# A decode block at the DMA rate: six units of K by transfers of eight rows, the second gate half ahead of the first's transposes, one stationary down block

## The chip, the cores and the metric

One core of a Trainium2 chip runs the whole program. The metric is the device time in microseconds, from runs on the chip. A profile comes from one further execution, taken by the hardware profiler. Engines are named as the profile names them: PE multiplies matrices, PEld loads PE's weights, DVE, ACT and POOL are the vector, scalar and general engines, SP is the queue that issues almost all transfers here. Sixteen DMA engines carry the transfers.

## The reference, cut to what matters

Two residual layers, each applied twice: grouped attention on a cache of 32768 positions (batch 2, 32 query heads, 8 key/value heads of width 128), then a gated feed-forward part. All data are float32. The two caches are 268 MB each and both are read in full in each of the two layers, 1074 MB in all; the weights are read beside them, and the only output is the result of 2 x 512 values.

```python
def _A_ref(x, k_cache, v_cache, wq, wo):
    q = (lambda x, *d: x.transpose(*d))((x @ wq).reshape(B, Sq, Hq, Dh), 0, 2, 1, 3)
    k = jnp.repeat(k_cache, rep, axis=1)
    v = jnp.repeat(v_cache, rep, axis=1)
    scores = jnp.einsum("bhqd,bhkd->bhqk", q, k) * (Dh ** -0.5)
    p = _softmax(scores, axis=-1)
    o = jnp.einsum("bhqk,bhkd->bhqd", p, v)
    ...
def _B_ref(x, w_gate, w_up, w_down):
    h = _gelu(g) * u          # g = x @ w_gate, u = x @ w_up
    return jnp.einsum("bsf,fd->bsd", h, w_down)

x = x + _A_ref(_layernorm(x, axis=-1), ...)
x = x + _B_ref(_layernorm(x, axis=-1), ...)
x = x + _A_ref(...)
x = x + _B_ref(...)
```

## The kernel before

**Memory.** `M` is one SBUF tile of 110 units; a unit is 512 columns (2 KB) in all 128 partitions. Three slots of 32 units (`SLOT_A`, `SLOT_B`, `SLOT_C`) take the chunks of K and V in turn. Three places of four units (`PL[0]`, `PL[1]`, `PL[2]`) take weights in pieces of four units. `mem(u, n)` is units u to u + n. A chunk of K or V is a half of one head's sequence: 32 units, 128 rows of 64 KB.

**Transfers.** `chunk` and `stream` only write a plan (`add`): an ordered list of key, source, place and size. `pump` (L101) issues from the head of that list on SP as long as the place is free, and stops at the first entry whose place is still taken. It is called by each `free`, that is at the point of the program where PE has been given the last instruction that reads the units. The order of the transfers is thus the order of the plan, and an entry that waits holds all behind it. Each transfer waits on SP until PE is done with its place.

**A layer.** For each of the 16 pairs of head g and batch b: `scores` runs two K chunks against the query window (L286), DVE takes the peak, `softmax` makes the weights and transposes them on PE (L305 to L320), `values` runs two V chunks (L330), `combine` and `project` add the head to the residual in the PSUM bank `W`. Layer 1 takes the pairs in the reverse order, and starts with the pair that layer 0 ended with: of its K, most of chunk 0 and all of chunk 1 are still there.

**The feed-forward part** (`feedforward`, L352). `center` takes the mean out of `W`; `deviation` gets the variance (PE L254, DVE, then a power on POOL). Gate and up weights are 28 units in two halves: `v = 0` has four column groups (16 units), `v = 1` three (12 units), each with four matmul steps over k (L367). Each half has a bank of its own, `G[0]` (bank 5) and `G[1]` (bank 7). Then ACT and DVE make the gelu product `th` of the half (L381 to L389), PE transposes it with `selt` (L391), DVE copies it to `hT` (L392). Only then does PE start the other half. `restart` (L230) puts the residual into `W` again, and the down product adds 14 blocks of 128 rows: as the moving operand against `hT` (L401), in the last layer only the first 10, and the last four as the stationary operand (`tail = 4`, L416), so that the result comes out transposed and needs no further step. In between, `halves` copies `W` out on ACT and DVE, and L408 sums its groups.

**Between the layers.** Weights pass through the three places: gate and up in seven pieces, down in four, the next queries in eight. The query of head 7 comes first (`Q7`, bank 5), since its K chunk 1 is in SBUF: `deviation(X)`, scaling (`query_copy`, L263 and L264), gather (L271) and `window`; then for each other group gg four query units (L259) into bank 7 and four units of scores (L286), and the score units' places are released for the next K pieces.

Of the kernel before, what the change touches and what calls it, by code (L numbers as in the profile page):

```python
# [16 lines left out]
P = 128  # L17
NB = 2
# [3 lines left out]
KC = DM // P  # L22
# [3 lines left out]
FD = DF // P  # L26
# [18 lines left out]
KFREE = CH - NPS  # L45

# [23 lines left out]
def block_kernel(ctx: ExitStack, tc: tile.TileContext, x, consts, kt, vt, wq, wo, gu, wd, out):  # L70
# [27 lines left out]
    def add(key, src, u, n):  # L98
        plan.append((key, src, u, n))

    def pump():  # L101
        while plan:
            key, src, u, n = plan[0]
            if any(busy[u:u + n]):
                return
            plan.popleft()
            for i in range(u, u + n):
                busy[i] = True
            live[key] = u
            nc.sync.dma_start(mem(u, n), src)  # L110
# [24 lines left out]
    def chunk(name, l, g, b, h, base, cuts=(CH,), turn=0):  # L135
        src = (kt if name == "k" else vt)[b, g, h]
        lo = 0
        where = {}
        for n in cuts:
            u = base + (lo + turn) % CH  # L140
            add((name, l, g, b, h, lo), cols(src, lo, n), u, n)
# [19 lines left out]
    for l in range(2):  # L161
# [190 lines left out]
    def feedforward(l):  # L352
# [5 lines left out]
        s = 0  # L358
        G = [bank[5], bank[7]]
        g, u, a, th = [mem(U_PT + j // 2)[:, (j % 2) * FN:(j % 2 + 1) * FN] for j in range(4)]  # L360
        for v in range(2):
            nt = 4 if v == 0 else 3
# [13 lines left out]
            R = 32 * nt  # L376
# [12 lines left out]
            nc.vector.tensor_tensor(th[:R], a[:R], u[:R], op=OP.mult)  # L389
            for j in range(2):  # L390
                nc.tensor.matmul(G[v][:, j * 8:(j + 1) * 8], th[:, j * P:(j + 1) * P], selt, start=True, stop=True)  # L391
            nc.vector.tensor_copy(hT[:, v].rearrange("p j r -> p (j r)"), G[v][:, :16])  # L392
        restart()
        where = pieces[("wd", l)]
        tail = 4 if l == 1 else 0
        for n in range(FD - tail):
            key, un = where[n]
            at(key)
            r, j = divmod(n, 2)
            v, t = divmod(r, 4)  # L400
            nc.tensor.matmul(W[32 * (n % 4):32 * (n % 4) + NB, :], hT[:, v, j, 2 * t:2 * t + NB], mem(un),  # L401
                             start=(0 < n < 4), stop=(n + 4 >= FD - tail))
            free(un)
        if tail:
            ws = mem(U_PT + 1)
            halves(ws, W)
            for c in (2, 3, 0, 1):
                nc.tensor.matmul(X[:, c * NB:(c + 1) * NB], ws[:, c * P:(c + 1) * P], sel[:, :NB],  # L408
                                 start=(c == 2), stop=False)
            for n in range(FD - tail, FD):  # L410
                key, un = where[n]
                at(key)
                r, j = divmod(n, 2)
                v, t = divmod(r, 4)
                for c in range(KC):
                    nc.tensor.matmul(X[:, c * NB:(c + 1) * NB], mem(un)[:, c * P:(c + 1) * P],  # L416
                                     hT[:, v, j, 2 * t:2 * t + NB], start=False,
                                     stop=(n == FD - 1 and c == KC - 1))
# [68 lines left out]
    for gg in range(7):  # L487
# [4 lines left out]
        if gg == 5:  # L492
            take(PL[1], 4) if False else None
        free(where[4 * gg][1], 4)
        n = 4 if gg < 6 else CH - i
# [87 lines left out]
```

## Time and profile before

| what | value |
|---|---|
| runs (us) | 2603.39, 2609.26, 2610.44; median 2609.26 |
| profiled execution, its own time | 2602.04 us |
| its span | 2599.9 us, 20241 instructions |
| PE granted clock, mean | 0.735 |
| busy: PE, PEld, DVE, ACT, POOL | 53%, 16%, 6%, 3%, 0% |
| HBM read | 1102.93 MB, 424 GB/s over the span |
| SP's data queue (q1) | 26496 packets, 1102.86 MB, 98.5% of 16 engines |

The span is the stretch from the first to the last instruction of the profiled execution; its own time also holds what lies around it. The profile's slices of the span give 428 to 440 GB/s, but for the first (421), the two around the middle (367 and 352) and the last (272). A row of the windows' view has, after the stretch and its length, the busy time of PE, PEld, DVE, ACT and POOL with the number of instructions, then PE's granted clock, the DMA engines' mean busy share (of 16) and GB/s. A row of the chain has the start, the length and what was done or waited for. A float32 matmul stands in the profile as two records, in the program's order as one.

### The profile page before, as it was taken

To read this page: it belongs to the slowest core of one execution; us is meant where nothing else is said; L and a number is where in the kernel's file an instruction comes from. 1 tells how busy PE (TensorE), PEld (TensorE's weight loads), DVE (VectorE), ACT (ScalarE), POOL (GpSimd) and SP (SyncE) were. 2 spreads that over 40 slices of the span, in tenths; PEclk is the share of its full clock that TensorE was granted. 3 is DMA by queue.
4 is the path that set the end of the run, shared out by engine and by line. 5 is a ranking of instruction groups with operands and counts; after the bars stand their busy time and mean duration, and the time that the engine had idled before them with its cause. 6 is when DMAs were issued, how large, how long until landed. Compare 5 with 4: busy or idle time off the path is not lost.

```text
span 2599.9 us, 20241 instructions
## 1 busy us (share of the span) xinstructions
PE 1370.0 (53%) x9456; PEld 409.2 (16%) x9456; DVE 147.2 (6%) x433; ACT 73.1 (3%) x196; POOL 3.2 (0%) x12
## 2 busy tenths in 40 slices
PE   3544544554554456445576554555455454455556
PEld 1111111111111111111122111111111111111112
DVE  0000000000000000000011000000000000000001
ACT  0000000000000000000000000000000000000000
POOL 0000000000000000000000000000000000000000
PEclk9776777677677767767788777776777777777767
DMA  9999999999999999999899999999999999999996
GB/s 421 434 433 434 432 434 429 433 435 434 430 433 431 429 435 435 431 433 434 367 352 440 431 433 430 434 434 433 434 431 431 432 430 434 434 433 434 431 428 272
DMA packets 26867, 1104.23 MB, mean 425 GB/s; under 512 B 3232, under 2 KB 3360, under 8 KB 4128
## 3 DMA queue, kind: packets, MB, share of 16 engines
q1 hardware_dynamic: 26496, 1102.86, 98.5%
q8 instruction: 74, 1.21, 0.2%
q10 hardware_dynamic: 288, 0.09, 0.0%
q14 instruction: 9, 0.07, 0.0%
HBM read 1102.93 MB, written 0.00 MB: 424 GB/s over the span
## 4 chain that ended last, share of the span: by engine, by line
DMA 58%; PE 28%; another core or an unknown queue 12%; DVE 1%; issue 1%; ACT 1%; SPq 0%; POOL 0%; ACTq 0%; DVEq 0%; POOLq 0%
DMA M<-in_vt 50%; PE bank L330 16%; PE bank L286 8%; DMA M<-in_kt 6%; DMA cst<-in_consts 1%; PE bank L348 1%; PE bank L341 1%; PE bank L367 1%; PE bank L259 1%; DVE M L235 0%; PE bank L401 0%; ACT M L234 0%; PE bank L416 0%; PE bank L242 0%
## 5 line engine op out<-in xcount | busy, mean ns | idle before, releaser
L286 PE MATMUL bank<-M,qw 128*32 128x512 f32 x4096 | 582.3, 731 | 534.8 <-DMA M<-in_kt 534.8
L330 PE MATMUL bank<-M 128*16 128x512 f32 x4096 | 580.1, 730 | 530.9 <-DMA M<-in_vt 530.9
L286 PEld LDWEIGHTS bank<-M,qw 128*32 128x32 f32 x4096 | 142.2, 131 | 963.7 <-DMA M<-in_kt 575.3
L330 PEld LDWEIGHTS bank<-M 128*16 128x16 f32 x4096 | 137.2, 112 | 947.2 <-issue 947.1
L289 DVE TENSOR_REDUCE sm<-bank 128x1 f32<-128x512 f32 x64 | 44.3, 692 | 1107.1 <-PE bank L286 1107.1
L311 ACT ACTIVATE M<-bank,sm 128x512 f32<-128x512 f32 x64 | 43.4, 682 | 1229.3 <-DVE sm L306 1229.3
L235 DVE COPY M<-bank 128x256 f32<-128x256 f32 x33 | 14.0, 425 | 1117.6 <-ACT M L234 1117.6
L314 PE MATMUL bank<-cst,M 128*128 128x128 f32 x256 | 49.2, 335 | 40.6 <-ACT M L311 40.3
L341 PE MATMUL bank<-cst,M 128*128 128x4 f32 x256 | 33.8, 255 | 30.4 <-DVE M L235 30.4
L315 DVE COPY M<-bank 128x512 f32<-128x512 f32 x64 | 43.8, 692 | 60.7 <-PE bank L314 60.7
L234 ACT COPY M<-bank 128x256 f32<-128x256 f32 x33 | 12.3, 372 | 1162.0 <-PE bank L330 1155.2
L314 PEld LDWEIGHTS bank<-cst,M 128*128 128x128 f32 x256 | 34.9, 169 | 51.6 <-ACT M L311 51.6
L341 PEld LDWEIGHTS bank<-cst,M 128*128 128x128 f32 x256 | 31.0, 191 | 59.9 <-DVE M L235 59.9
L305 PE MATMUL bank<-cst,sm 128*128 128x128 f32 x32 | 10.3, 323 | 35.0 <-DVE sm L304 35.0
L348 PE MATMUL bank<-M,oT 128*2 128x512 f32 x128 | 21.1, 736 | 4.1 <-DVE oT L343 4.1
L259 PE MATMUL bank<-M,xw 128*32 128x512 f32 x128 | 21.2, 777 | 3.7 <-DMA M<-in_wq 3.0
L319 PEld LDWEIGHTS bank<-cst,sm 128*128 128x128 f32 x128 | 21.8, 240 | 0.0
L367 PE MATMUL bank<-M,xw 128*32 128x512 f32 x112 | 20.4, 785 | 2.1 <-DMA M<-in_gu 1.6
L319 PE MATMUL bank<-cst,sm 128*128 128x4 f32 x128 | 20.1, 263 | 0.0
L230 PE MATMUL bank<-cst,xin 128*2 128x128 f32 x40 | 6.0, 301 | 23.4 <-DMA cst<-in_consts 23.4
L305 PEld LDWEIGHTS bank<-cst,sm 128*128 128x128 f32 x32 | 4.2, 133 | 64.1 <-DVE sm L304 64.1
L311 ACT ACTIVATION_READ_ACCUMULATOR M<-bank,sm 128x1 f32 x64 | 12.5, 196 | 0.0
(70 smaller groups left out, 150.4 us busy)
## 6 DMA issues: line engine op xcount, KB each, us to landing
M<-in_wo SPq DMA_DIRECT2D x16, 1024.0 KB, 51.1
M<-in_vt SPq DMA_DIRECT2D x2, 6144.0 KB, 46.6
M<-in_wq SPq DMA_DIRECT2D x2, 4096.0 KB, 17.1
M<-in_gu SPq DMA_DIRECT2D x8, 1024.0 KB, 6.4
M<-in_wq SPq DMA_DIRECT2D x8, 1024.0 KB, 6.4
M<-in_kt SPq DMA_DIRECT2D x2, 4096.0 KB, 18.8
M<-in_kt SPq DMA_DIRECT2D x6, 1024.0 KB, 13.2
M<-in_gu SPq DMA_DIRECT2D x3, 2048.0 KB, 44.5
```

What stands on the lines that cost most here:

```text
L259: nc.tensor.matmul(Q[32 * k:32 * k + 32, :], xw[:, k, XO - 2 * g:XO - 2 * g + 32], mem(u), start=start, stop=stop)
L286: nc.tensor.matmul(S[32 * t:32 * t + 32, :], w[:, 28 - 4 * c:60 - 4 * c], mem(u), start=start, stop=stop)
L289: nc.vector.tensor_reduce(mx[:, h:h + 1], S, axis=AX.X, op=OP.max)
L305: nc.tensor.transpose(X[:, :P], nm.to_broadcast([P, P]), ident)
L311: nc.scalar.activation(p[h], S[h], AF.Exp, bias=bias, scale=SCALE, accum_out=ls[:, h:h + 1])
L314: nc.tensor.transpose(S[h][:, k * P:(k + 1) * P], p[h][:, k * P:(k + 1) * P], ident)
L315: nc.vector.tensor_copy(mem(U_PT + h), S[h])
L319: nc.tensor.matmul(X[:, P:P + REP], ls[:, h:h + 1].to_broadcast([P, P]), mask, start=(h == 0), stop=(h == 1))
L330: nc.tensor.matmul(acc[32 * t:32 * t + 16, :], mem(U_PT + h)[:, k * P + 32 * t + 16 * e:k * P + 32 * t + 16 * e + 16], mem(u), start=(h == ...
L341: nc.tensor.matmul(X[:, :REP], md[:, c * P:(c + 1) * P], sel[:, 4 * c:4 * c + 4], start=(c == 2), stop=(c == 1))
L348: nc.tensor.matmul(W[32 * t:32 * t + NB, :], oT[:, t, :], mem(u + t), start=(t > 0 and g == orders[l][0][0]), stop=(g == orders[l][-1][0]))
L367: nc.tensor.matmul(G[v][32 * t:32 * t + 32, :], xw[:, k, XO:XO + 32], mem(un), start=(k == 0), stop=(k == KC - 1))
```

## The change

It has four parts.

1. `LOW` names two K chunks per layer. For them `pump` issues the transfer as three: rows 0 to 111, 112 to 119 and 120 to 127. In each layer one chunk is named whole (32 units) and of the other only its first half (16 units); 16 rows of 48 units are as many bytes as 128 rows of six units. The bytes and places are the same.
2. `feedforward` gives PE the products of the second half before the transposes of the first. The restart, the first transposes, eight down blocks, the second transposes and the other blocks follow.
3. In the last layer one down block, not four, is the stationary operand (`tail = 1`), and it comes before the sum over `W`'s groups.
4. Between the layers the variance of the query goes to `W` and not to `X`, so that the first other group's query units run before the gather of head 7; scores follow from the second group on, five units a time.

```diff
+LOW = [{(3, 1): (CH,), (6, 0): (CH // 2, CH // 2)}, {(4, 0): (CH,), (1, 1): (CH // 2, CH // 2)}]
...
-            key, src, u, n = plan[0]
+            key, src, u, n, rows = plan[0]
...
-            nc.sync.dma_start(mem(u, n), src)
+            lo = 0
+            for m in rows:
+                nc.sync.dma_start(mem(u, n)[lo:lo + m], src[lo:lo + m])
+                lo += m
...
-            chunk(nm_, l, g, b, h, ring[i % 3], (24, 4, 4) if last else (CH,))
+            cuts, rows = (CH,), (P,)
+            if last:
+                cuts = (24, 4, 4)
+            elif nm_ == "k" and h == 0 and (g, b) in LOW[l]:
+                cuts, rows = LOW[l][(g, b)], (P - 16, 8, 8)
+            chunk(nm_, l, g, b, h, ring[i % 3], cuts, rows=rows)
...
+        products(0)
+        gelu(0)
+        products(1)
+        restart()
+        hidden(0)
+        gelu(1)
+        down(0, 8)
+        hidden(1)
+        down(8, FD)
         if tail:
             ws = mem(U_PT + 1)
             halves(ws, W)
+            for n in range(FD - tail, FD):
+                key, un = below[n]
+                at(key)
+                for c in range(KC):
+                    nc.tensor.matmul(X[:, c * NB:(c + 1) * NB], mem(un)[:, c * P:(c + 1) * P], part(n),
+                                     start=(n == FD - tail and c == 0), stop=False)
             for c in (2, 3, 0, 1):
                 nc.tensor.matmul(X[:, c * NB:(c + 1) * NB], ws[:, c * P:(c + 1) * P], sel[:, :NB],
-                                 start=(c == 2), stop=False)
+                                 start=False, stop=(c == 1))
...
-    deviation(X)
+    deviation(W)
     query_copy(Q7, mem(U_PT))
-    query_gather(mem(U_PT), Q7, 7, 1)
-    w = window(g, b)
...
+        if gg == 0:
+            query_gather(mem(U_PT), Q7, 7, 1)
+            w = window(g, b)
+            continue
+        n = 5 if gg < 6 else CH - i
```

`products`, `gelu` and `hidden` are the three pieces of the old loop over `v` (L362 to L375, L376 to L389, L390 to L392) as functions; `down(lo, hi)` is the loop of L396 to L403 over blocks lo to hi, up to the stationary ones.

PE, the feed-forward part of layer 0 and the start of layer 1. Before (bank_79 is bank 5, bank_80 `W`, bank_81 bank 7, also called `X`; L242 and L244 belong to `center`, L254 is the variance):

```order
L367 MATMUL bank_79<-M,xw 32x512 x12
L391 MATMUL bank_79<-cst,M 128x8 x2
L367 MATMUL bank_81<-M,xw 32x512 x12
L391 MATMUL bank_81<-cst,M 128x8 x2
L230 MATMUL bank_80<-cst,xin 2x128 x4
L401 MATMUL bank_80<-M,hT 2x512 x14
L242 MATMUL bank_81<-cst,M 128x4 x4
L244 MATMUL bank_81<-cst,sm 128x16 x2
L259 MATMUL bank_79<-M,xw 32x512 x4
L254 MATMUL bank_81<-sm 128x2
L271 MATMUL bank_79<-cst,M 128x2 x4
L259 MATMUL bank_81<-M,xw 32x512 x4
```

Now (line numbers of the changed kernel: L379 is L367 before, L407 L391, L242 the restart, L422 L401, L271 L259, L266 L254, L283 L271):

```order
L379 MATMUL bank_79<-M,xw 32x512 x12
L379 MATMUL bank_81<-M,xw 32x512 x12
L242 MATMUL bank_80<-cst,xin 2x128 x4
L407 MATMUL bank_79<-cst,M 128x8 x2
L422 MATMUL bank_80<-M,hT 2x512 x8
L407 MATMUL bank_81<-cst,M 128x8 x2
L422 MATMUL bank_80<-M,hT 2x512 x6
L254 MATMUL bank_81<-cst,M 128x4 x4
L256 MATMUL bank_81<-cst,sm 128x16 x2
L271 MATMUL bank_79<-M,xw 32x512 x4
L266 MATMUL bank_80<-sm 128x2
L271 MATMUL bank_81<-M,xw 32x512 x4
```

The second half's products and the restart moved ahead of the first transposes, eight down blocks ahead of the second transposes, and (last row) the first other group's query units ahead of the gather, which stood in this place.

PE at the end of the program, before:

```order
L367 MATMUL bank_81<-M,xw 32x512 x12
L391 MATMUL bank_81<-cst,M 128x8 x2
L230 MATMUL bank_80<-cst,xin 2x128 x4
L401 MATMUL bank_80<-M,hT 2x512 x10
L408 MATMUL bank_81<-cst,M 128x2 x4
L416 MATMUL bank_81<-hT,M 128x2 x16
L578 UNCONDITIONAL_BRANCH
```

Now (L442 is L416 before, L445 L408):

```order
L379 MATMUL bank_81<-M,xw 32x512 x12
L242 MATMUL bank_80<-cst,xin 2x128 x4
L407 MATMUL bank_79<-cst,M 128x8 x2
L422 MATMUL bank_80<-M,hT 2x512 x8
L407 MATMUL bank_81<-cst,M 128x8 x2
L422 MATMUL bank_80<-M,hT 2x512 x5
L442 MATMUL bank_81<-hT,M 128x2 x4
L445 MATMUL bank_81<-cst,M 128x2 x4
L606 UNCONDITIONAL_BRANCH
```

Sixteen stationary matmuls became four, three blocks went to the moving operand, and the stationary ones stand ahead of the sum over groups.

SP in layer 0, around the K chunk of head 3, batch 1. Now:

```order
L114 DMA M<-in_kt 128x16384 x2
L114 DMA M<-in_vt 128x16384 x2
L114 DMA M<-in_kt 112x16384
L114 DMA M<-in_kt 8x16384 x2
L114 DMA M<-in_kt 128x16384
L114 DMA M<-in_vt 128x16384
```

Before, the third and fourth of these rows and the fifth were two transfers of 128 rows. SP has 123 rows for 113, ten more transfers in all.

ACT's and DVE's instructions stand in the same order as before (one DVE instruction reads its variance from `W` instead of `X`). On DVE the copy of the first transposes to `hT` still stands ahead of the second half's elementwise work.

More of the change, by code (lines that the diff above doesn't have):

```diff
@@ L133, in block_kernel, with chunk @@
     pieces = {}
-    def chunk(name, l, g, b, h, base, cuts=(CH,), turn=0):
+    def chunk(name, l, g, b, h, base, cuts=(CH,), turn=0, rows=(P,)):
         src = (kt if name == "k" else vt)[b, g, h]
@@ L392, in feedforward, with part, down @@
             nc.vector.tensor_copy(hT[:, v].rearrange("p j r -> p (j r)"), G[v][:, :16])
[L393 to L398, printed above, removed]
+        below = pieces[("wd", l)]
+        tail = 1 if l == 1 else 0
+        def part(n):
             r, j = divmod(n, 2)
             v, t = divmod(r, 4)
-            nc.tensor.matmul(W[32 * (n % 4):32 * (n % 4) + NB, :], hT[:, v, j, 2 * t:2 * t + NB], mem(un),
-                             start=(0 < n < 4), stop=(n + 4 >= FD - tail))
-            free(un)
+            return hT[:, v, j, 2 * t:2 * t + NB]
+        def down(lo, hi):
+            for n in range(lo, min(hi, FD - tail)):
+                key, un = below[n]
+                at(key)
+                nc.tensor.matmul(W[32 * (n % 4):32 * (n % 4) + NB, :], part(n), mem(un),
+                                 start=(0 < n < 4), stop=(n + 4 >= FD - tail))
+                free(un)
+        products(0)
[7 more added lines that the diff above has]
+        down(8, FD)
         if tail:
@@ L406, in feedforward @@
             halves(ws, W)
+            for n in range(FD - tail, FD):
+                key, un = below[n]
+                at(key)
+                for c in range(KC):
+                    nc.tensor.matmul(X[:, c * NB:(c + 1) * NB], mem(un)[:, c * P:(c + 1) * P], part(n),
+                                     start=(n == FD - tail and c == 0), stop=False)
             for c in (2, 3, 0, 1):
                 nc.tensor.matmul(X[:, c * NB:(c + 1) * NB], ws[:, c * P:(c + 1) * P], sel[:, :NB],
-                                 start=(c == 2), stop=False)
[L410 to L418, printed above, removed]
+                                 start=False, stop=(c == 1))
             y = sm[:, 0:8]
```

20 lines of the change are left out of this document (10 added, 10 removed).

## The prediction

> **What bounds the kernel now.** I read the page's totals first, then busy time by stage, then the chain of work that ended last at the two places where the transfers stop.
>
> From the page: the queue of instruction fetches, and the chain's shares.
>
> ```profile
> q8 instruction: 74, 1.21, 0.2%
> DMA 58%; PE 28%; another core or an unknown queue 12%; DVE 1%; issue 1%; ACT 1%; SPq 0%; POOL 0%; ACTq 0%; DVEq 0%; POOLq 0%
> ```
>
> By stage (busy time of each engine, PE's granted clock, the DMA engines' mean busy share, GB/s):
>
> ```profile
> 1400.00:2540.00 1140.00, 584.88 (x4067) 168.56 (x4063) 59.11 (x162) 26.90 (x74) 0.00 (x0) 0.73 1.00 433
> 1310.00:1314.00 4.00, 4.00 (x24) 0.90 (x18) 0.00 (x0) 0.00 (x0) 0.00 (x0) 0.77 0.37 104
> 1314.00:1334.00 20.00, 11.73 (x69) 4.63 (x66) 3.92 (x17) 2.47 (x7) 0.55 (x1) 0.79 0.96 369
> 1334.00:1340.00 6.00, 6.00 (x34) 2.23 (x37) 0.34 (x2) 0.00 (x0) 0.00 (x0) 0.57 0.48 164
> 1286.00:1287.00 1.00, 1.00 (x16) 0.35 (x12) 0.00 (x0) 0.00 (x0) 0.00 (x0) 1.00 0.58 229
> 1287.00:1292.00 5.00, 4.00 (x40) 1.54 (x28) 0.42 (x1) 0.37 (x1) 0.00 (x0) 1.00 0.50 210
> 1292.00:1293.00 1.00, 0.75 (x9) 0.13 (x9) 0.16 (x1) 0.00 (x0) 0.00 (x0) 1.00 0.27 115
> 2568.00:2573.00 5.00, 4.87 (x30) 1.33 (x26) 0.17 (x2) 0.00 (x0) 0.55 (x1) 0.67 1.00 411
> 2574.00:2579.00 5.00, 2.93 (x22) 1.29 (x25) 1.88 (x7) 0.89 (x2) 0.31 (x1) 1.00 0.49 202
> 2580.00:2581.00 1.00, 0.21 (x3) 0.00 (x0) 0.23 (x1) 0.47 (x1) 0.00 (x0) 1.00 0.21 78
> ```
>
> Inside a layer the 16 DMA engines are busy throughout (1.00, 433 GB/s) and PE for half of it: only bytes, or their sharing out, count there. Time can be saved where the share falls: between the layers, and after the last transfer. The rows at 1287 and 2574 show more. The share does not fade, it stands at a half (0.50, 0.49), for 6.5 us between the layers (half the engines are done by about 1286.2, where the share is at 0.58, the other half by 1292.7) and 6.1 us at the end (2573.7 to 2579.9). I read this as eight engines that fall behind the other eight by that much in each layer. The instruction fetches (1.21 MB beside the data) would do it if they run on eight engines only; the row gives no engine.
>
> The chain between the layers, and SP's issues there (start, us, what; L367 gate and up, L391 transposes of a half, L401 down, L259 queries, L254 their variance, L271 their gather):
>
> ```profile
> 1299.22 4.79 DMA M<-in_gu
> 1304.06 1.11 PE bank L367 x8
> 1308.30 0.89 PE bank L391 x4
> 1309.19 4.93 PE bank L367 x24
> 1320.38 4.45 DMA M<-in_wd
> 1328.82 1.92 PE bank L259 x8
> 1330.74 0.53 PE bank L254 x2
> 1333.24 1.87 PE bank L271 x8
> 1339.90 4.76 DMA M<-in_wq
> 1348.32 18.11 DMA M<-in_kt
> ...
> 1312.38 8.32 SPq L110 DMA_DIRECT2D M<-in_wd  x4
> 1322.12 21.54 SPq L110 DMA_DIRECT2D M<-in_wq  x8
> 1345.83 39.69 SPq L110 DMA_DIRECT2D M<-in_kt  x11
> ```
>
> A weight piece is issued when PE has consumed the piece in its place, and lands 4.8 us after that (4.79, 4.76); PE then waits for it. A loop of PE and DMA leaves the DMA engines idle for 4 x 0.63 + 20 x 0.04 + 6 x 0.52 = 6.4 us from 1310 to 1340. Once the K transfers start (1345.83) they are the bound again, so what is saved before that is saved at the end.
>
> The end of the chain (L381 and L389 first and last of a half's elementwise work, L230 the restart of the residual, L408 the sum over groups, L416 the stationary blocks):
>
> ```profile
> 2568.97 3.96 PE bank L367 x24
> 2573.03 0.48 ACT M L381
> 2575.49 0.44 DVE M L389
> 2576.07 0.58 PE bank L391 x4
> 2576.65 3.60 PE bank L367 x24
> 2580.27 0.48 ACT M L381
> 2583.28 0.58 PE bank L391 x4
> 2583.87 0.85 PE bank L230 x7
> 2584.72 4.41 PE bank L401 x17
> 2590.11 1.05 PE bank L408 x8
> 2591.16 6.12 PE bank L416 x32
> 2597.31 0.17 DVE sm L420
> ...
> L416 PE MATMUL bank<-hT,M 128*128 128x2 f32 x32 | 6.2, 330 | 0.0
> L401 PE MATMUL bank<-M,hT 128*2 128x512 f32 x20 | 4.6, 908 | 0.0
> ```
>
> PE stands still from 2572.93 to 2576.07 and from 2580.25 to 2583.28 while ACT and DVE work on a half, with nothing of the other half to do. A matmul is two records: a down block costs 2 x 0.23 = 0.46 us as the moving operand (4.6 / 20 each) and 8 x 0.195 = 1.55 us as the stationary one (6.2 / 32).
>
> **The end, layer 1.** From the end of the first half's products (2572.93) to the copy (2597.31) is 24.4 us. The new chain on PE: second half's products 3.6, restart 0.9, first transposes 0.58, their copy to SBUF and the step to the next matmul 0.6 (in the rows this lies under the restart, so it is 0.9 at most), eight down blocks 3.7, second transposes 0.58, copy again 0.6, five blocks 2.3, the one stationary block 1.55 with the ACT and DVE halves (about 1.0) beside it, sum over groups 1.05, a step 0.1: 15.6 us. **Gain 8.8 us.** Cover: the first half's elementwise work (2573.03 to 2575.93) lies under the 3.6 us of products. The second half's does not start freely: DVE's copy of the first transposes stands ahead of it and waits for PE, until about 2578.6; 2.4 us of DVE and ACT work (from the end of L381 at 2580.75 to 2583.15 now) end at 2581.0, and PE reaches the second transposes at 2582.4, so 1.4 us are spare. If that cover goes, the wait falls on the second transposes. The weights arrive in time: the transfers end at about 2581 (share 0.21 there). Ends: 7 (PE slower by a tenth) and 10 us.
>
> **Between the layers.** The second half's products now start when their piece lands (about 1306.7, behind the one of 1304.0) rather than at 1309.19, but their last piece lands no earlier: its place is freed by the first half at 1305.1, and two pieces of 2.5 us are in the queue ahead of it (1304.0 + 3 x 2.5 = 1311.6). So they end about 0.7 us sooner, and the first transposes (1308.30), now queued behind them on PE, come 6 us later. This alone would gain nothing. What gains is the release: the piece in the first down place is consumed near 1309.2 instead of 1312.3, so SP issues the down weights 3.1 us earlier; eight blocks run before the second transposes, and the layer's end and the query's start (1328.82) come **3.3 us earlier**. Then the query: now PE waits from 1331.3 to 1333.24 for scale and copy, gathers, and only then runs the first other group. After the change that group runs in the wait (the variance goes to W, which is free, so X is not held), and two pieces are released earlier; five scores a round cost 0.26 us more each. I get 1340.8 for the first K issue, 5 us earlier. Ends: 0 (the new order only shifts the wait onto the same pieces) and 6.4 (all idle time gone). I take **5**, nearer the upper end since each release time above comes from a row.
>
> The orders on record show ten more transfers on SP, at 0.33 us each:
>
> ```profile
> 1401.07 0.33 SPq L110 DMA_DIRECT2D M<-in_vt  x1
> ```
>
> They stand behind the same slot as the transfer that they replace, with tens of us of queued transfers ahead: nothing on the path.
>
> **Eight rows.** 433 GB/s over 16 engines is 27.1 a piece: a row of a K chunk (64 KB) takes 2.42 us. Now each engine has eight rows. With 112 + 8 + 8, every engine has seven, and eight engines one or two more: for a full and a half chunk per layer, eight engines get 3.63 us more and the others 3.63 less. No row here shows a transfer of eight rows, so it is bounded: on the leaders, the laggards end 3.6 us earlier, the leaders 6.5 - 3.6 = 2.9 earlier than the laggards did; the last engine counts, and as a half's edges are up to 1 us wide I take **2.3 us a layer, 4.6 in all**. On the laggards, 3.6 us later a layer. Spread over both halves, 0. I take the leaders: the shift of 7.25 us between the halves is nearest to the 6.5 and 6.1 that the rows show. [...]
>
> **Sum.** 8.8 + 5 + 4.6 = 18.4 us off the profiled execution's own 2602.0 (span 2599.9 and 2.1 around it): 2583.6. The median of the runs shown lies 7.2 above that execution, so 2590.8 for a median.
>
> **Rivals.**
> - *The eight-row transfers clog.* Eight neighbouring rows are two groups of four partitions. If four engines that write into one such group share what one has now, a row takes 4 x 2.42 = 9.7 us. Two transfers in the full chunk and two half ones cost the eight engines 21.8 us a layer on top of 3.6; less their lead of 6.5 and 6.1, the layers end 18.9 and 19.3 us later: 38.2 - 13.8 = 24.4 slower, about 2633.7, more if the 112 rows collide too. It decides once a 64 KB row costs more than about 5.6 us: 3 x (5.6 - 2.42) + 3.6 - 6.3 = 6.9 a layer eats the 13.8. For it: the full rate is only shown where 128 rows are written at once. Against it: no row shows one engine held up by another. [...] 18%.
> - *The laggards get the rows.* 7.3 us lost against 13.8: 6.5 faster, about 2602.7. 10%.
> - *The shift does nothing* (the rows are dealt out to both halves, or the last landing isn't what PE waits for): 13.8 faster, about 2595.4. The second is unlikely, as DMA holds 58% of the chain. 12%.
> - *The forecast*, 60%; its own range 2582 to 2599, from the ends of its three terms and the run-to-run scatter (2603.39 to 2610.44).
>
> The clock does not decide: PE is granted 0.73 in the streams, where it waits anyhow.
>
> Chances: a difference of about 0.3% (7.8 us) is what these runs can tell from none. Faster takes the forecast, the idle shift and a third of the wrong half: 0.75; same 0.07; slower the clog, 0.18. The range must reach the wrong half and keep the scatter: 2577 to 2611, leaving out the clog.
>
> **What would show it.** At the two ends of the stream the share should fall from 1.00 to 0 within 2 to 3 us, with no stretch at 0.50; a stretch at 0.50 of over 10 us means the wrong half; K landings of the four chunks later by 10 us or more, with the share under 1.00 there, mean the clog. Between the layers, SP's first K issue should come about 5 us sooner after the last V landing, and the share from 1310 to 1346 lose most of its idle time. At the end, the copy should follow the first half's products by about 15.6 us, and the second half's products should follow the first's without a gap. A second-transposes wait on DVE over 1.5 us would say that the cover was too thin.

## The result and the profile after

The changed kernel takes 2729.53 us (median of 4 runs, 2724.01 to 2731.71) against 2609.85 for the one before (4 runs, 2603.39 to 2611.48): ratio 1.046, 95% interval 1.0436 to 1.0484. The forecast was 2590.8, and the range left this out. The profiled execution has a span of 2729.1 us.

The page's DMA and GB/s lines (40 slices of the span), after:

```profile
DMA  9999999999999999999789999999999999999997
GB/s 424 436 429 430 436 434 431 436 287 350 435 430 433 435 358 344 431 432 436 333 331 438 432 433 432 434 433 430 211 432 431 436 433 427 274 431 432 433 429 299
```

The same line of before:

```profile
GB/s 421 434 433 434 432 434 429 433 435 434 430 433 431 429 435 435 431 433 434 367 352 440 431 433 430 434 434 433 434 431 431 432 430 434 434 433 434 431 428 272
```

Four dips are new: slices 9 and 10, 15 and 16, 29, 35, at the four K pieces that the change splits. The DMA digits still say 9: the engines are busy there and move less. By windows of after (columns as in the prediction; last two DMA share and GB/s):

```profile
535.00:640.00 105.00, 34.91 (x233) 11.19 (x237) 3.30 (x10) 1.82 (x5) 0.00 (x0) 0.63 1.00 287
575.00:580.00 5.00, 1.15 (x8) 0.37 (x12) 0.00 (x0) 0.00 (x0) 0.00 (x0) 0.50 0.98 210
600.00:625.00 25.00, 0.00 (x0) 0.00 (x0) 0.00 (x0) 0.00 (x0) 0.00 (x0) 0.50 0.96 102
980.00:1060.00 80.00, 28.65 (x197) 8.26 (x189) 3.28 (x10) 1.82 (x5) 0.00 (x0) 0.66 1.00 292
```

Against 433 GB/s the first and last row lose 105 x (1 - 287/433) = 35.4 and 80 x (1 - 292/433) = 26.1 us, 61.5 in layer 0. Inside, the rate first stands at 210 (575 to 580: the 112 rows), then at 102 (600 to 625: the eight-row transfers and what the other engines do meanwhile). The share stays near 1.00, so it is each row that takes longer: worked out from the rate for 16 engines, a row of 64 KB takes 2.4 us at 433 GB/s, 5.0 at 210 and 10.3 at 102.

Where the 129 us lie, from the chain that ended last and SP's issues. V's last chunk of a layer comes in pieces of 24, 4 and 4 units; its row here is the piece of 24, which lands at start plus length (the last piece lands some 5 us later). L254 is the first step after the residual, L448 the copy. After:

```profile
1305.55 46.47 DMA M<-in_vt
1417.80 23.31 SPq L114 DMA_DIRECT2D M<-in_kt  x9
2643.94 47.74 DMA M<-in_vt
2705.19 1.13 PE bank L254 x8
2726.37 0.17 DVE sm L448
```

Before (L242 is that first step):

```profile
1236.12 45.27 DMA M<-in_vt
2502.75 48.03 DMA M<-in_vt
2563.98 1.40 PE bank L242 x8
```

| stretch | before | after | difference |
|---|---|---|---|
| start to the landing of V's 24 units, layer 0 | 1281.39 | 1352.02 | +70.6 |
| from there to layer 1's first K issue | 64.4 | 65.8 | +1.3 |
| from there to the landing of V's 24 units, layer 1 | 1204.95 | 1273.88 | +68.9 |
| from there to the copy | 46.5 | 34.7 | -11.8 |

So the end gained, the stretch between the layers did not, and each layer's stream lost about 70 us. In layer 0, 61.5 of these 70.6 lie at the two split pieces; the other 9 aren't taken apart. One sign may bear on them. After V the share was to fall with no stretch at 0.50. In after it reads:

```profile
1348.00:1350.00 2.00, 0.00 (x0) 0.00 (x0) 0.00 (x0) 0.00 (x0) 0.00 (x0) 1.00 0.54 225
1350.00:1363.00 13.00, 9.84 (x65) 2.25 (x65) 0.42 (x1) 0.37 (x1) 0.00 (x0) 0.74 0.12 49
```

The stretch at a half is short now, but 13 us at 0.12 follow, as if two of the 16 engines (0.12 x 16 = 1.9) were far behind. With the clog in the same layer, neither can be put down to the shift of load that was forecast.

### The profile page after: what moved, and what is told of

Read it like the earlier page. It is cut to its first block, busy times and chain, and to the rows that moved or that the text cites. A ratio compares the mean times of both kernels' runs of the same rounds, so it can differ in the third digit from the quotient of the medians.

```text
span 2729.1 us, 20231 instructions
## 1 busy us (share of the span) xinstructions
PE 1372.0 (50%) x9438; PEld 404.0 (15%) x9438; DVE 147.0 (5%) x433; ACT 73.2 (3%) x196; POOL 3.3 (0%) x12
## 4 chain that ended last, share of the span: by engine, by line
DMA 52%; PE 27%; another core or an unknown queue 19%; DVE 1%; issue 1%; ACT 0%; SPq 0%; ACTq 0%; DVEq 0%
DMA M<-in_vt 45%; PE bank L342 16%; PE bank L298 8%; DMA M<-in_kt 6%; PE bank L353 1%; PE bank L360 1%; DMA M<-in_wq 1%; PE bank L379 1%; DMA M<-in_gu 0%; DMA M<-in_wd 0%; PE bank L326 0%; DVE M L247 0%; ACT M L246 0%; PE bank L422 0%
## 5 line engine op out<-in xcount | busy, mean ns | idle before, releaser
L298 PE MATMUL bank<-M,qw 128*32 128x512 f32 x4096 | 590.6, 736 | 629.6 <-DMA M<-in_kt 629.6
L342 PEld LDWEIGHTS bank<-M 128*16 128x16 f32 x4096 | 137.0, 112 | 989.4 <-issue 989.4
L317 PE MATMUL bank<-cst,sm 128*128 128x128 f32 x32 | 10.3, 322 | 35.0 <-DVE sm L316 35.0
L379 PE MATMUL bank<-M,xw 128*32 128x512 f32 x112 | 21.4, 767 | 5.6 <-DMA M<-in_gu 5.1
L271 PE MATMUL bank<-M,xw 128*32 128x512 f32 x128 | 19.0, 698 | 3.8 <-DMA M<-in_wq 3.1
L242 PE MATMUL bank<-cst,xin 128*2 128x128 f32 x40 | 6.0, 300 | 23.3 <-DMA cst<-in_consts 23.3
(70 smaller groups left out, 137.0 us busy)
## 6 DMA issues: line engine op xcount, KB each, us to landing
M<-in_kt SPq DMA_DIRECT2D x6, 1024.0 KB, 13.6
```

The costliest lines, as they stand in the source:

```text
L271: nc.tensor.matmul(Q[32 * k:32 * k + 32, :], xw[:, k, XO - 2 * g:XO - 2 * g + 32], mem(u), start=start, stop=stop)
L298: nc.tensor.matmul(S[32 * t:32 * t + 32, :], w[:, 28 - 4 * c:60 - 4 * c], mem(u), start=start, stop=stop)
L317: nc.tensor.transpose(X[:, :P], nm.to_broadcast([P, P]), ident)
L342: nc.tensor.matmul(acc[32 * t:32 * t + 16, :], mem(U_PT + h)[:, k * P + 32 * t + 16 * e:k * P + 32 * t + 16 * e + 16], mem(u), start=(h == ...
L379: nc.tensor.matmul(G[v][32 * t:32 * t + 32, :], xw[:, k, XO:XO + 32], mem(un), start=(k == 0), stop=(k == KC - 1))
```

## The experiments

**The rows alone, and all but the rows.** The first kernel is the one before with the diff's `LOW`, `add`, `pump` and `chunk`; the second is the changed one with

```
-LOW = [{(3, 1): (CH,), (6, 0): (CH // 2, CH // 2)}, {(4, 0): (CH,), (1, 1): (CH // 2, CH // 2)}]
+LOW = [{}, {}]
```

> The kernel before, with the rows (112 + 8 + 8 for the four K pieces) and nothing else of the change. Theory 1 (the rows are the whole loss): the windows of the changed kernel lose 36 us at the full piece (565 to 635) and 24 us at the half one, 120 us in two layers, and some 15 more at the layers' ends where its 16 engines land apart: 2735 to 2750, the changed kernel's 2729.5 plus the about 14 that the two other parts gain. Theory 2 (the new order between the layers or at the end costs time too): under 2720, as the rest of the change then explains part of the loss.

> The changed kernel with every K piece in one transfer of 128 rows again; gate half, transposes, query order and the one stationary block stay. Theory 1 (the prediction's two other terms hold, 8.8 at the end and 5 between the layers): 2596 against 2609.85 before, ratio 0.9947; the copy follows the first half's products by 15.6 us, and K is issued 5 us sooner after the last V landing. Theory 2 (only the end holds, the order between the layers moves its waits onto the same pieces): 2601, ratio 0.9966. Theory 3 (the order is a loss): 2610 or more.

Measured: the rows alone 2742.14 us, ratio 1.0513 (1.0494 to 1.0533); all but the rows 2591.55, ratio 0.994 (0.9926 to 0.9954). The rows are the whole loss, as theory 1 has it: 137.0 us, and the rest of the change is a gain of 13.6. For all but the rows the time fits theory 1 (ratio 0.9947), but its two signs fail: the copy comes 12.8 us after the first half's products, not 15.6, and K is issued no sooner (66.8 us after V's 24 units, for 64.4 before). Between the layers theory 2 is nearer to what happened; the end gained more than either theory had, and the sum came out by luck.

**112 + 16 in place of 112 + 8 + 8**, on the kernel before:

```
-                cuts, rows = LOW[l][(g, b)], (P - 16, 8, 8)
+                cuts, rows = LOW[l][(g, b)], (P - 16, 16)
```

> The kernel before, with its four K pieces as 112 + 16 rows in place of 112 + 8 + 8; nothing else of the change. It parts the 112 rows' share of the loss from that of the eight rows. Theory 1 (engines that write into the same partitions' group share one's rate): the 112 rows run at half rate (210 against 433 GB/s) and lose 18 and 9 us a layer, 54 in all; the 16 rows lie in four groups and take 9.7 us for 2.4, 22 in all: +76, about 2686. Theory 2 (only transfers that use eight engines are slow): the 16 rows lose nothing and the 112 rows keep their half rate: +54, about 2664. Theory 3 (the 112 rows were only slow because eight rows followed them): within 10 us of the time before, about 2610.

Measured 2706.16, ratio 1.0386 (1.0363 to 1.041): +101, near no theory. The eight-row form is 36 us of the loss; 101 stay when the rest goes in one transfer of 16 rows.

**Transfers by themselves.** A probe computes nothing of the reference; each form is issued, waited for and followed by the next:

```
+    for d, s in parts: nc.sync.dma_start(M[d, 0:CH * U], a[s])
+    nc.vector.tensor_copy(mark, M[:, 0:1])
```

> Computes nothing of the reference: it moves 64 KB rows of K into SBUF in one form after the other, each form alone and waited for by a one-column DVE copy. Forms in order: 128 rows, 112 rows, 8 rows into neighbouring partitions (112 to 119), 8 rows into every fourth partition (0, 4, .. 28) from neighbouring rows of K, 8 rows into neighbouring partitions from every fourth row of K, 16 rows, 64 rows, 32 rows, 96 rows, 120 rows, 112 + 8 + 8, 8 rows at a step of 16 in both, 16 rows at a step of 8 in both, 128 rows. Theory 1 (engines that write into the same eight partitions share what one has, 27.1 GB/s): 128 rows 19.4 us at 433 GB/s; 8 neighbouring rows are two groups of four and take 4 x 2.42 = 9.7 us, wherever they come from; 8 rows in every fourth partition 2.4 us; 16 neighbouring rows 9.7 us at any number of engines; 112 rows more than 7 x 2.42 = 17 us, about 35 as in the changed kernel. Theory 2 (what is shared lies on the reading side, by the address in HBM): 8 rows into every fourth partition from neighbouring rows 9.7 us, 8 neighbouring partitions from every fourth row 2.4 us. Theory 3 (nothing is shared; the long rows of the changed kernel come from transfers that run beside each other): each form alone takes its rows per engine x 2.42 us: 8 rows 2.4 us, 112 rows 17 us, 120 rows 17 to 19 us, and only 112 + 8 + 8 takes longer than its parts.

The chain of waits of the first probe; in order 128, 112, 8 neighbouring rows, 8 rows into every fourth partition, 8 neighbouring partitions from every fourth row of K, 64, 96 and 120 rows, and the last part of 112 + 8 + 8:

```profile
1.16 21.92 DMA M<-in_kt
23.28 32.72 DMA M<-in_kt
56.28 11.20 DMA M<-in_kt
67.76 5.11 DMA M<-in_kt
73.14 11.10 DMA M<-in_kt
...
96.58 23.21 DMA M<-in_kt
...
133.01 31.87 DMA M<-in_kt
...
165.15 42.51 DMA M<-in_kt
...
208.67 48.93 DMA M<-in_kt
```

Theory 1 for the eight rows: 11.2 us into neighbouring partitions and 5.1 into every fourth, and it makes no difference from where they are read (11.1). Without 2.5 us around a transfer (an estimate: 128 rows took 21.9 us, and are 19.4 at 433 GB/s), a row costs 8.7 us in place of 2.6; the rival in the prediction had said 9.7. 112 rows take 30.2 us for 17, more than the 19.4 of 128 rows, and 120 take 40.

> Computes nothing of the reference: as the first probe, 64 KB rows of K into the same partitions, each form alone and waited for. Forms in order: 128 rows; one row at partition 0; one at 4; one at 64; 8 rows at a step of 4 from 0, from 4, from 64; 16 rows at a step of 4 from 0, from 32; 112 rows from 16; 48 rows; 80 rows; 64 + 64 rows in two transfers; four transfers of 32 rows at a step of 4; 128 rows. About 2.5 us of each time lie outside the rows (21.9 against 19.4 for 128 rows in the first probe). It asks why in the first probe every row of 96, 112 and 120 rows took about 5 us, also where no second engine should write into its group. [...] Theory 2 (an engine has its full rate only into its own group, the one it writes in a transfer of 128 rows, and half of it into others): row 4 and row 64 7.4 us, 8 rows from 4 and from 64 7.4 us, from 0 5 us; 16 rows from 32 5 us. [...]

Of the second probe: one row at 0, 4 and 64; eight rows every fourth partition from 0, 4 and 64; 16 rows every fourth from 0 (to 60) and from 32 (to 92); 48 rows; then, from SP's last issue, 64 + 64 rows and four transfers of 32 rows, every fourth partition:

```profile
23.46 4.73 DMA M<-in_kt
28.47 4.53 DMA M<-in_kt
33.27 4.46 DMA M<-in_kt
38.00 5.22 DMA M<-in_kt
43.49 5.13 DMA M<-in_kt
48.89 5.05 DMA M<-in_kt
54.22 7.52 DMA M<-in_kt
62.01 5.32 DMA M<-in_kt
...
100.74 26.93 DMA M<-in_kt
...
156.20 42.81 DMA M<-in_kt
...
201.13 20.48 DMA M<-in_kt
```

Theory 2 fails: a row cost the same at the three places (4.73, 4.53 and 4.46 us), eight rows too (5.22, 5.13 and 5.05), where it has 7.4 from 4 and from 64. What counts is which partitions are written together: 16 rows took 7.52 us from 0 to 60 and 5.32 from 32 to 92, nearly double without the 2.5 us of each outside the rows. Two halves of 64 rows take twice as long as the whole (42.81 us from the last issue, for 21.92), and four combs of 32 rows take no longer than the whole (20.48). One form stands apart: 48 rows took 26.9 us, more than the 23.2 of 64 rows; how a transfer deals its rows to the engines stays open. The expectations count groups of partitions; an estimate from these times fits their numbers, 16 in all, since the 16 rows from 32 to 92 took hardly longer than eight, and eight under 64 neighbouring rows, since these moved at about 200 GB/s (4.19 MB in 23.21 - 2.5 us), about half of 433. Which partitions make up a group was not shown.

**Split without the clog, in the kernel.** A first try, on the changed kernel, went wrong in a way worth showing:

```
-                cuts, rows = LOW[l][(g, b)], (P - 16, 8, 8)
+                cuts, rows = LOW[l][(g, b)], [slice(j, j + 125, 4) for j in range(4)]
```

> The changed kernel with the same four K pieces split into four transfers of 32 rows each, every fourth partition (0, 4, .. 124; 1, 5, ..; and so on), in place of 112 + 8 + 8; all else as changed. It asks whether the split costs, or the partitions that each part holds. In the second probe four such transfers moved 128 rows at the full rate. Theory 1 (the partitions decide: each of these transfers reaches all 16 groups): as without the rows, 2591.5 within 3, and the windows at the four pieces show 433 GB/s. Theory 2 (any split of a piece costs, as engines fall out of step): 2640 or more. Theory 3 (full rate within a piece, but collisions at its borders where some engines still are in the transfer before): 2 to 5 us a piece, 2600 to 2612.

Measured 2630.3, ratio 1.0083 (1.007 to 1.0097), near no theory. Two windows, and one thing that DVE waited for between 480 and 700 (us in total, times, longest):

```profile
560.00:590.00 30.00, 0.00 (x0) 0.00 (x0) 0.00 (x0) 0.00 (x0) 0.00 (x0) 0.50 1.00 433
590.00:607.00 17.00, 10.82 (x76) 4.49 (x80) 1.77 (x5) 1.45 (x4) 0.00 (x0) 0.64 0.08 32
DVE M L315 <- DMA M<-in_kt: 48.0, 1, 48.0
```

The piece runs at full rate, and PE does nothing; then the queue is dry for 17 us. DVE's step of the softmax (L315, which writes into one unit of the big tile) waited 48 us for the landing of a K piece that it doesn't use, and without the softmax no place comes free for the next transfer. It is as if rows at a step were taken as the whole span of the one big tile. With a tile for each slot of 32 units, and one for the rest, instead,

```
-    M = cp.tile([P, NU * U], F32, name="M")
+    Ms = [cp.tile([P, (min(lo + CH, NU) - lo) * U], F32, name=f"M{lo // CH}") for lo in range(0, NU, CH)]
```

three more kernels: the same four combs; two combs, `slice(j, j + 127, 2)`; two halves, `slice(j, j + 64)`.

> The kernel with four transfers of 32 rows, every fourth partition, for each of the four K pieces (2630.3 with one big tile), with one tile for each place. Theory 1 (the 39 us were DVE's wait for a landing that it doesn't use, which made values and places late and the queue run dry for 17 us a piece): as without the rows, 2591.5 within 3. Theory 2 (the queue ran dry because SP can't hold that many transfers): still 2620 or more.

> The changed kernel with the four K pieces as two transfers of 64 rows each, every second partition (0, 2, .. 126 and 1, 3, .. 127), in place of 112 + 8 + 8; the big tile is cut into one tile for each place, so that no engine waits for a landing that it doesn't use. Theory 1 (the partitions decide; each transfer reaches all 16 groups): as without the rows, 2591.5 within 3, and 433 GB/s at the four pieces. Theory 2 (any split costs, as engines fall out of step): about as two_halves, 2650 or more. Theory 3 (each engine's four rows still share groups, as a transfer deals its rows to the engines in an order that isn't known): in between, 2 to 20 us a piece.

> The same with two transfers of 64 neighbouring rows (0 to 63 and 64 to 127). Theory 1 (the partitions decide; each half reaches eight groups, two engines to a group): 64 + 64 rows took 43 us for 20.5 in the second probe, so 20 and 10 us a layer more for a full and a half piece, 60 in all, and 10 to 20 after it as the engines land apart: 2650 to 2670. Theory 2 (16 engines work through both transfers side by side and fill all groups): as two_every_second.

Measured: four combs 2590.37, ratio 0.9941 (0.9927 to 0.9954); two combs 2592.16, ratio 0.9948 (0.9934 to 0.9962); two halves 2672.28, ratio 1.0253 (1.0238 to 1.0268). Theory 1 holds for the two kernels with combs: no loss against 2591.55, and with the four combs DVE's wait is gone too. The halves lie just above its 2670. Two combs, then two halves, at the full piece of layer 0:

```profile
560.00:590.00 30.00, 16.18 (x120) 4.48 (x112) 0.59 (x2) 0.37 (x1) 0.00 (x0) 0.73 1.02 440
```

```profile
575.00:600.00 25.00, 9.41 (x72) 3.03 (x72) 0.59 (x2) 0.37 (x1) 0.00 (x0) 0.70 1.00 208
```

This is the cleanest pair: as many transfers, rows and bytes, and 80 us between them from the partitions alone. The DMA share is 1.02 and 1.00.

**Two that told little.** To see what a shift of load between the engines is worth, six column units of a K piece per layer went by 16 eight-row transfers, as combs or as neighbours (`EIGHTS`, on the kernel without the rows):

```
+EIGHTS = [slice(i + j, i + j + 29, 4) for i in (0, 32, 64, 96) for j in range(4)]
+EIGHTS = [slice(i, i + 8) for i in range(0, P, 8)]
```

> The kernel without the rows, with six of the 32 column units of one K piece per layer moved by 16 transfers of eight rows, the rows in every fourth partition (0, 4, .. 28; 1, 5, ..) so that each row of a transfer lies in a group of its own. If such a transfer runs on eight engines, these get 8 x 12 KB = 3.63 us more and the other eight 3.63 less, the shift that the prediction wanted. Theory 1 (what is shared is the group of partitions, and each group's share of the bytes is unchanged, so no split over engines gains): no clog, 2591.5 within 3. Theory 2 (engines are the limit and the leaders get the rows): 2.3 a layer faster, 2587. Theory 3 (the laggards get them): 3.6 a layer slower, 2599. Theory 4 (any transfer of eight rows clogs): 20 or more a layer, over 2630.

> The same six column units by 16 transfers of eight neighbouring rows each (0 to 7, 8 to 15, ..): as many transfers, rows and bytes as with the stride, only the partitions of a transfer lie in two groups of four. Theory 1 (four engines that write into a group share one's rate): each transfer takes 4 x 0.45 = 1.81 us for 0.45, 29.0 us on eight engines in place of 7.3, 19 to 25 us a layer: 2630 to 2642. Theory 2 (the 112 rows were the cause of the clog in the changed kernel, or only 64 KB rows clog): as with the stride, within 3.

Measured 2631.42 for the combs, ratio 1.0091 (1.0078 to 1.0105), and 2608.13 for the neighbours, ratio 1.0002 (0.9993 to 1.0011). The combs, of the one big tile, have DVE's wait again (52.9 us, once, for a landing of K), so the pair compares nothing.

The neighbours lost 16.6 us against the kernel without the rows, less than half of what was expected; SP, which had to wait for landings of K before it could issue some of the 16 (16 times, 60.2 us, between 500 and 660; 4 times, 39.7 us, without the rows), has a share in it that isn't known.

**The other two parts.** `end_only` is the kernel before with the new order and the one stationary block in layer 1 alone; `ff_only` is the kernel without the rows and with the query order of before.

```
+        if l == 0:
+            for v in range(2): products(v); gelu(v); hidden(v)
+            restart(); down(0, FD)
```

> The kernel before with the new order of the gate, up and down part and the one stationary block in layer 1 only; layer 0's part, the query order and the 128-row transfers stay as before. Theory 1 (the end carries the whole gain: 33.3 us from the first transposes of the residual to the copy before, 21.2 in the kernel without the rows): 12 faster than before, 2593, with no difference from the kernel without the rows that can be told. Theory 2 (layer 0's new order costs the about 2 us that the trace without the rows shows between V's last landing and the first K issue): 2590. Theory 3 (layer 0's new order gains 5 as predicted, and the end only 8.8): 2596.

> The kernel without the rows, with the query order of before (gather before the next group, four scores a round); the gate, up and down part is new in both layers. Theory 1 (the query order moves its waits onto the same pieces of wq: query start to first K issue takes 17.0 us in both traces): 2591.5, as without the rows. Theory 2 (the query order gains and layer 0's new gate order hides it): 3 to 5 slower than without the rows, and the first K issue comes 20 us after the query start.

Measured 2593.8, ratio 0.9946 (0.9933 to 0.996), and 2591.6, ratio 0.9938 (0.9926 to 0.9951). Both stand with the kernel without the rows (0.994): the end carries the gain, and neither layer 0's order nor the query order adds anything that these runs can tell. The theories of `end_only` lie 3 us apart and its runs cover 2590.57 to 2594.34, so its time doesn't choose among them; in its trace the end takes 21.2 us, as without the rows.

**Sizes.** `tail = 4` again; and in layer 0 the second transposes after four down blocks (`first = 8 if l == 1 else 4`), both on the kernel without the rows.

> The kernel without the rows, with four stationary down blocks at the end as before, not one; nothing else. It sizes the one-block part of the end's gain. Theory 1 (the prediction's prices, 1.55 us for a stationary block and 0.46 for a moving one): 3 x 1.09 = 3.3 slower than without the rows, 2595. Theory 2 (the prices of the trace without the rows: 0.98 and 0.38): 3 x 0.6 = 1.8 slower, 2593.4. Theory 3 (the weights' landing hides it): 2591.6.

> The kernel without the rows, with layer 0's second transposes after four down blocks, not eight, so that they lie in the wait for the second piece of down weights (3.55 us ahead of block 5 there); layer 1 keeps eight. Theory 1 (transposes and copy then leave the chain between the layers): 0.97 + 0.27 = 1.2 faster than without the rows, 2590.4; query start 1.2 earlier after the residual's transposes (34.9 to 33.7 us). Theory 2 (they wait for the second half's elementwise work and hold up block 5): 0 to 1 slower.

Measured 2593.96, ratio 0.9952 (0.9939 to 0.9965), and 2588.64, ratio 0.9935 (0.9923 to 0.9947). Neither is told apart from 0.994. The traces are finer: with four stationary blocks the stretch from the residual's first transposes to the copy takes 24.8 us for 21.2, near the 3.3 of theory 1; with the earlier second transposes the query starts 34.0 us after the residual's transposes for 34.9, 0.9 of the 1.2 expected. `early_second` has the lowest median of all kernels here, 16 us below the one before; that it beats the kernel without the rows isn't shown.

## Why the prediction was wrong, step by step

**Eight rows: the step that failed.** It priced the parts of a split piece by the row of a whole one, "a row of a K chunk (64 KB) takes 2.42 us", for the 112 rows ("every engine has seven") and the eight. That price held for some sets of partitions and not for others: alone, 16 rows took 5.32 us into every fourth partition from 32 to 92, and 7.52 from 0 to 60. The transfers of 128 rows had the rate (433 GB/s) and so had the combs (433 and 440), runs of fewer neighbours did not: alone, a row of the 112 takes 30.2 / 7 = 4.3 us (an estimate, with seven rows an engine) and one of the eight 8.7. Expected was a gain of 4.6; measured are 137 us of loss (2742.14 against 2605.12). That eight engines, the same for both transfers of eight rows, get one or two rows more, from which the 2.3 us a layer come, no run shows; the runs show the 137 us, and 11.2 us for eight neighbouring rows alone. For the eight rows the partitions are the cause, as the probe shows (11.2 us for neighbours, 5.1 for every fourth). That the 112 rows are slow for the same reason is an estimate, from their rate (210 GB/s) and from the halves against the combs (208 against 440); which engine takes which of the 112 rows was not found. What a shift of load between the halves is worth was not seen by itself: the form that should carry no clog had other waits.

**The clog rival** looked for the cause in the partitions, had the price of the eight rows (9.7, measured 8.7), and got 18%. It gave 24.4 us, since it left the 112 rows at their full rate and said only "more if the 112 rows collide too". They ran at 210 GB/s, and in the kernel a split piece cost more than alone: 112 + 8 + 8 takes 49.7 us in the probe (from the first issue at 207.93) for 21.9, 27.8 more, and 35.4 in the stream. What it meets there is not taken apart. Its sign was half wrong as well: the share did not fall under 1.00 (1.00 from 535 to 640). "Against it: no row shows one engine held up by another" was weak evidence: the K, V and weight transfers of the kernel before all write 128 rows, so none of its rows could show it.

**The end: right, and too small.** Forecast 8.8 (7 to 10). From the residual's first transposes to the copy it took 33.3 us before and 21.2 after (rows above): 12.1 us less, and 21.2 to 22.3 in every kernel with the new end and one stationary block. The chain of waits at the end without the rows, and two rows of PE (eight down blocks, second transposes):

```profile
2570.53 7.85 PE bank L379 x48
...
2583.28 1.88 PE bank L422 x10
2585.15 0.98 PE bank L442 x8
...
2587.23 0.17 DVE sm L448
```

```profile
2580.06 1.90 PE L422 MATMUL bank<-M,hT 128*2 128x512 f32 x16 [0.27 <-DVE hT L408]
2582.43 0.58 PE L407 MATMUL bank<-cst,M 128*128 128x8 f32 x4 [0.47 <-DVE M L403]
```

The second half's products follow without a gap, as said. Half of x48 belongs to the first half, so from its end (about 2570.53 + 3.93) to the copy are 12.8 us, for 15.6. The eight blocks took 1.90, not 3.7, the five 1.88, not 2.3, and the stationary one 0.98, not 1.55. Why shows in the granted clock (third number from the end). Before: a stretch at full clock, then the down blocks and the stationary blocks:

```profile
2572.00:2584.90 12.90, 6.63 (x59) 2.73 (x50) 4.66 (x14) 2.72 (x6) 0.31 (x1) 1.00 0.39 157
2584.70:2589.10 4.40, 4.40 (x22) 1.08 (x13) 0.00 (x0) 0.00 (x0) 0.00 (x0) 0.61 0.00 0
2591.20:2597.20 6.00, 6.00 (x32) 5.98 (x31) 0.00 (x0) 0.00 (x0) 0.00 (x0) 0.55 0.00 0
```

Without the rows, up to the copy; and with four stationary blocks (`tail_4`), the last of them:

```profile
2574.00:2587.20 13.20, 12.19 (x94) 5.25 (x86) 4.99 (x15) 3.09 (x7) 0.31 (x1) 1.00 0.34 137
```

```profile
2587.60:2590.20 2.60, 2.60 (x13) 2.57 (x13) 0.00 (x0) 0.00 (x0) 0.00 (x0) 0.50 0.00 0
```

The prices were measured at 0.61 and 0.55 and spent at 1.00. Both kernels have 13 us at full clock here. Before, PE stood still for half of them (busy 6.63 us) and the down blocks ran after them; without the rows the whole end fits in (busy 12.19). With four stationary blocks it doesn't, and the last of them run at 0.50. So, by the author's estimate, about 2.8 of the 12.1 us (12.8 for 15.6) come from a clock that the prediction left out, and "The clock does not decide" was wrong at the end. The cover was thinner than forecast: as the eight blocks took 1.8 us less, the second transposes waited 0.47 us for DVE where 1.4 were to spare; the sign of over 1.5 was not reached.

**Between the layers: the release came, the gain didn't.** From the landing of V's 24 units to the first K issue it took 64.4 us before, and 65.8 with everything changed; without the rows 66.8 (V, SP's issues, then the residual's first transposes and the query on PE):

```profile
1235.77 45.70 DMA M<-in_vt
1310.65 7.98 SPq L114 DMA_DIRECT2D M<-in_wd  x4
1348.27 36.40 SPq L114 DMA_DIRECT2D M<-in_kt  x11
1296.42 1.87 PE L254 MATMUL bank<-cst,M 128*128 128x4 f32 x8 [1.04 <-DVE sm L252]
1331.30 1.78 PE L271 MATMUL bank<-M,xw 128*32 128x512 f32 x8 [0.26 <-DVE xw L258]
```

In `tail_4`, which is the same up to there, it took 63.6, so this stretch scatters by 3 us between runs of the same program. The forecast was 5 us less. The step that failed is "the layer's end and the query's start (1328.82) come **3.3 us earlier**". From the residual's first transposes (1294.47 before, 1296.42 now) the query starts after 34.4 us before and 34.9 now, 0.5 later. PE before, the transposes and the last blocks, then without the rows (in brackets the idle time ahead, and what ended it):

```profile
1294.47 1.63 PE L242 MATMUL bank<-cst,M 128*128 128x4 f32 x8 [1.06 <-DVE sm L240]
1323.72 2.18 PE L401 MATMUL bank<-M,hT 128*2 128x512 f32 x12 [1.69 <-DMA M<-in_wd]
```

```profile
1321.83 1.88 PE L422 MATMUL bank<-M,hT 128*2 128x512 f32 x8 [3.55 <-DMA M<-in_wd]
1323.64 1.02 PE L407 MATMUL bank<-cst,M 128*128 128x8 f32 x4
1324.93 3.44 PE L422 MATMUL bank<-M,hT 128*2 128x512 f32 x12 [0.27 <-DVE hT L408]
```

SP issued the down weights at 1310.65, not 1312.38, and PE got on 1.9 us earlier, though the trace came to this part 1.95 us later; counted from the residual's transposes the release came 3.7 us sooner (3.1 forecast). But before, six blocks were left then, 2.2 us; now it is ten blocks and the second transposes, 6.5 us. What was moved out of the products' gaps went behind a wait for weights. The clock has a part in it: the last six blocks took 2.18 us before and 3.44 now, at a granted clock of 1.00 and 0.52. The query order gained nothing either, as `ff_only` says.

**The 60% for the forecast** rested on the eight rows only lightly, 4.6 of 18.4 us. Without them the sum is the rival "the shift does nothing", a gain of 13.8, and 13.6 was measured (2605.12 to 2591.55). That is luck: the end gave 3.3 more than forecast, partly by the clock, and the stretch between the layers gave nothing for 5. The error was to let a part worth 4.6 at best go in with a price that no row had tested, and a known way to lose far more.

## What to carry to other kernels

Give each part of a split transfer every second or every fourth partition, not a run of neighbours (here 2592.16 and 2590.37 us, for 2672.28 with two halves); and read GB/s beside the DMA share, which stood at 1.00 in the halves at 208 GB/s. Where a tile is shared by many pieces, rows at a step can bring waits that the order of the work doesn't need (48.0 us for DVE here), and the row "DVE <- DMA" names them; a tile for each slot took them away here. Before moving work ahead of a wait, ask what then stands behind the last landing, and at which clock the prices were taken.

## What was not expected of the hardware

Transfers of 96, 112 and 120 neighbouring rows took longer than one of 128 (31.9, 32.7 and 42.5 us for 21.9), although they move less; which engine takes which row was not found. If an engine has eight of the 120 rows, a row takes 40 / 8 = 5.0 us, an estimate. PE's granted clock at the end stood at 1.00 for 12.9 us before and for 13.2 without the rows, with PE busy for 6.63 and 12.19 us of them. After that it was 0.61 and 0.55 in the two stretches of before, and 0.50 in the last 2.6 us with four stationary blocks, while PE worked throughout; what sets that time is open.
